# 128 rows of B's output weights by transfers of 5, 3 and 4 partitions

## The chip, the cores and the metric

The kernel runs on one core of a Trainium2 chip. Its time is the device time of one execution in microseconds (us). Before the change the median of 3 runs is 246.3 us (246.22 to 246.44). The profile is of one more execution; its span, from its first instruction to its last, is 245.2 us, and all positions below count from the start of that span.

## The reference

Two independent decode steps of attention, A and B, with one query token each; the two output rows are put side by side. For A only the last 2,048 of the 8,192 cached positions count, for B all of them.

```python
# per side: x [1,1,576], k_cache and v_cache [1,16,8192,128], wq [576,4096], wo [4096,576]
q = (x @ wq).reshape(B, Sq, Hq, Dh)              # 32 heads of 128, two for each cached head
scores = einsum("bhqd,bhkd->bhqk", q, k) * Dh ** -0.5
p = softmax(scores)
o = einsum("bhqk,bhkd->bhqd", p, v)
out = o.reshape(B, Sq, 4096) @ wo                # [1, 1, 576] for each side
```

All inputs are bf16. Nearly all the work is to read 102.8 MB once from HBM.

## The kernel before

**Loads.** Every large input goes through one ring in SBUF, `ring`, of 72 x 1,024 bf16 elements in each of 128 partitions. The helper `place` takes the next stretch of the ring and makes the load wait for the last use of what lay there. All loads are issued by SyncE (SP) in one order: wq of A and B, then K and V of eight units (four units of four cached heads for A, four for B), and at last wo. Each is one transfer over 128 partitions, and the profile's DMA records show it as 8 packets (one for each partition) on each of 16 DMA engines, each engine's share closed by a 4-byte packet that counts the semaphore up by one. An engine works through its packets in order, so the loads queue up behind one another by tens of us.

**Attention.** For each unit VectorE (DVE) turns slabs of K (line 350), TensorE (PE) makes the scores (line 367; a unit of A has a mask matmul of 4 partitions in front, line 359), ScalarE (ACT) takes the exponential (line 406), DVE turns that (lines 414 and 418), and PE multiplies by V (line 431), as the slabs land. Line 447 folds the result into `ob`.

**The end.** Lines 482 to 499 divide o by the softmax's sums and turn it, so that `oP[p, P, k]` holds number 32p + k of side P's o. wo has the same layout: partition p holds the 32 rows 32p to 32p + 31. One "row k" of the ring is thus 128 rows of wo, one in each partition, 576 elements (1,152 bytes) each. Line 229 loads wo: A's in one transfer of 32 rows, B's in five transfers of 17, 8, 4, 2 and 1 rows (`NWO`, line 34). For each row, PE makes two matmuls (line 510) with one column of `oP` as the stationary side: 320 output columns into one partition of the PSUM bank `fb`, 256 into another. A uses partitions 0 and 32 of `fb`, B 64 and 96. A matmul group waits for its own transfer and comes in program order: F0.0 (A, 32 rows), then F1.0 to F1.4 (B, 17, 8, 4, 2 and 1 rows). When a side is done, ACT (line 519) and DVE (line 521) copy its two sums to `outsb`, and SP stores 1,152 bytes (line 523). The store of A's row is issued behind all loads, and so is B's, which ends the program.

**Order.** Each engine runs its own list in program order; `op` adds an instruction with the names that it waits for, `load` a transfer with its semaphore.

Of the kernel before, what the change touches and what calls it, by code (L numbers as in the profile page):

```python
# [4 lines left out]
BF16 = mybir.dt.bfloat16  # L5
# [6 lines left out]
HQ = 32  # L12
G = 16
DH = 128
DM = 576
# [5 lines left out]
NQ = G // 4  # L21
# [8 lines left out]
N0 = 320  # L30
RING = 72 * 1024
NSEM = 24
NKT = 3
NWO = [[32], [17, 8, 4, 2, 1]]


class Prog:
# [9 lines left out]
    def op(self, eng, fn, deps=(), name=None):  # L47
        self.ops[eng].append((fn, tuple(deps), name, None))
        if name is not None:
            assert name not in self.where, name  # L50
            self.where[name] = (eng, len(self.ops[eng]) - 1)

    def load(self, eng, fn, sem, value, deps=(), name=None, step=16):
        self.ops[eng].append((fn, tuple(deps), None, (sem, step)))
        if name is not None:
            assert name not in self.dma, name
            self.dma[name] = (sem, value)
# [40 lines left out]
def bass_concat_heads__sliding_block_cached__gqa_block_cached__decode_kernel(nc, A_x, A_k_cache, A_v_cache, A_wq, A_wo,  # L98
                         B_x, B_k_cache, B_v_cache, B_wq, B_wo, out):
    xs, ks, vs = [A_x, B_x], [A_k_cache, B_k_cache], [A_v_cache, B_v_cache]  # L100
    wqs, wos = [A_wq, B_wq], [A_wo, B_wo]
# [4 lines left out]
    ring = nc.alloc_sbuf_tensor("ring", [128, RING], BF16)  # L106
    ktb = nc.alloc_sbuf_tensor("ktb", [128, NKT * SLAB], BF16)
    ident = nc.alloc_sbuf_tensor("ident", [128, 128], BF16)
# [33 lines left out]
    on = nc.alloc_sbuf_tensor("on", [128, 2, HQ], BF16)  # L142
    oq = nc.alloc_sbuf_tensor("oq", [128, 2, HQ], BF16)
    oP = nc.alloc_sbuf_tensor("oP", [128, 2, HQ], BF16)
    warm = nc.alloc_sbuf_tensor("warm", [128, 8], F32)
    outsb = nc.alloc_sbuf_tensor("outsb", [1, 2 * DM], BF16)

# [3 lines left out]
    mb = nc.alloc_psum_tensor("mb", [128, 512], F32)  # L151
    ob = nc.alloc_psum_tensor("ob", [128, 512], F32)

    def view(t, free, offset, dims, parts=128, p0=0):
        return bass.AP(tensor=t, offset=p0 * free + offset, ap=[[free, parts], *dims])

    pg = Prog(nc)
    op, load = pg.op, pg.load
    s_x = [nc.alloc_semaphore("s_x%d" % i) for i in range(2)]
    s_ld = [nc.alloc_semaphore("s_ld%d" % i) for i in range(NSEM)]  # L160
    s_out = nc.alloc_semaphore("s_out")
    s_row = [nc.alloc_semaphore("s_row%d" % i) for i in range(2)]


    live, at, nload, uses_of = [], [0], [0], []

    def place(size, uses, issue, name):
        if at[0] + size > RING:
            at[0] = 0
        lo, hi = at[0], at[0] + size  # L170
        at[0] = hi
        deps = []
        for r in list(live):
            if r[0] < hi and lo < r[1]:
                deps += r[2]
                live.remove(r)
        n = nload[0]
        nload[0] += 1
        if n >= NSEM:
            deps += uses_of[n - NSEM]  # L180
        uses_of.append(list(uses))
        live.append((lo, hi, list(uses)))
        t = ring[:, lo:hi]
        load("sp", lambda e: issue(e, t), s_ld[n % NSEM], 16 * (n // NSEM + 1), deps=deps, name=name)
        return t
# [39 lines left out]
    for P in range(2):  # L225
        k0 = 0
        for c, kk in enumerate(NWO[P]):
            src = wos[P].rearrange("(p k) n -> p (k n)", k=HQ)[:, k0 * DM:(k0 + kk) * DM]
            wo_at[P, c] = place(kk * DM, ["F%d.%d" % (P, c)], lambda e, t, src=src: e.dma_start(t, src),
                                "wo%d.%d" % (P, c))  # L230
            k0 += kk

    def slab(kind, i, s):

        parts = kv_at[kind, i]
        per = nslab[i] // len(parts)
        return parts[s // per][:, s % per * SLAB:(s % per + 1) * SLAB], "%s%d.%d" % (kind, i, s // per)
# [6 lines left out]
       deps=["id0"], name="ident")  # L244
# [12 lines left out]
    op("pool", lambda e: e.memset(zb[:], 0.0), name="zb0")  # L257
    op("pool", lambda e: e.tensor_copy(mkr[:], view(ident, 128, 0, [[0, 128], [1, 4]], 4)), deps=["ident"], name="mkr")
    op("pool", lambda e: e.memset(pts[:], 0.0), name="pts0")
    for c in range(2):  # L260
        op("dve", lambda e, c=c: e.tensor_reduce(par[:, c:c + 1], view(identf, 128, c, [[2, 64]]), AX.X, ALU.add),
           deps=["identf"], name="par%d" % c)
# [3 lines left out]
    for P in range(2):  # L266
        op("dve", lambda e, P=P: e.tensor_copy(  # L267
            view(xdup, 256, 128 * P, [[2, 64], [1, 2]], parts=1),
            view(xrow, 2 * DM, P * DM + 512, [[1, 64], [0, 2]], parts=1)), deps=["x%d" % P], name="xd%d" % P)
        for k in range(5):  # L270
            def mm(e, P=P, k=k):
                if k < 4:
                    lhsT = view(xrow, 2 * DM, P * DM + k, [[4, 128]], parts=1)
                else:
                    lhsT = xdup[0:1, P, :]
                return e.matmul(banks[2 * P + k // 4][:, (k % 4) * 128:(k % 4 + 1) * 128], lhsT=lhsT,  # L276
                                rhs=onesb[0:1, :], start=True, stop=True)
            op("pe", mm, deps=["x%d" % P, "onesb", "xd%d" % P], name="xT%d.%d" % (P, k))
        op("dve", lambda e, P=P: e.tensor_copy(
            xrep[:, P, 0:4, :].rearrange("p k m -> p (k m)"), banks[2 * P][:, :]), deps=["xT%d.3" % P], name="xr%d.0" % P)  # L280
        for c in range(2):
            op("dve", lambda e, P=P, c=c: e.tensor_scalar(
                xrep[:, P, 4 + c, :], banks[2 * P + 1][:, 0:128], par[:, c:c + 1], None, ALU.mult),
                deps=["xT%d.4" % P, "par%d" % c], name="xr%d.%d" % (P, 1 + c))
# [3 lines left out]
       deps=["identf"], name="clsb")  # L288
    op("dve", lambda e: e.tensor_reduce(clsa[:], view(identf, 128, 0, [[1, 8], [8, 16]]), AX.X, ALU.add),
       deps=["identf"], name="clsa")  # L290
    op("dve", lambda e: e.tensor_reduce(sel[:], view(identf, 128, 0, [[1, 32], [32, 4]]), AX.X, ALU.add),
       deps=["identf"], name="sel")
# [6 lines left out]
    for P in range(2):  # L299
        for n in range(8):  # L300
# [3 lines left out]
            def mm(e, P=P, n=n, bank=bank):  # L304
# [8 lines left out]
               name="qmm%d.%d" % (P, n))  # L313
            op("act", lambda e, u=u, bank=bank: e.activation(qsb[:, u % 4, :], bank[:, :], ACT.Copy),  # L314
               deps=["qmm%d.%d" % (P, n)] + (["qT%d" % (u // 2 - 2)] if u >= 4 else []), name="qe%d" % u)
            if n % 2:
# [3 lines left out]
                    deps=["qe%d" % (u - 1), "qe%d" % u] + (["z0.%d" % i for i in range(4)] if P else []),  # L320
                    name="qT%d" % (u // 2))
        for b in range(4):
            if P == 1:
# [3 lines left out]
                    deps=["qT%d" % u for u in range(4, 8)] + ["zb0"], name="z1.%d" % b)  # L327
            else:
# [3 lines left out]
                    deps=["qT%d" % u for u in range(4)] + ["za0"], name="z0.%d" % b)  # L332
# [4 lines left out]
    k0 = [sum(nslab[:i]) for i in range(NU)]  # L337
# [117 lines left out]
    for i in range(NU):  # L455
        n = nslab[i + 1] if i + 1 < NU else 0
# [18 lines left out]
        for s in range(nslab[i]):  # L475
# [13 lines left out]
                                start=True, stop=True),  # L489
       deps=["lsel", "lselA", "nb%d" % last, "mr%d" % last], name="L")  # L490
# [3 lines left out]
        deps=["rl", "O%d" % last], name="on")  # L494
    op("dve", lambda e: e.transpose(oq[:].rearrange("p c k -> p (c k)"), on[:].rearrange("p c k -> p (c k)")),
       deps=["on"], name="oq")
    op("pe", lambda e: e.matmul(mb[:, 64:128], lhsT=perm[:, :], rhs=oq[:].rearrange("p c k -> p (c k)"),
                                start=True, stop=True), deps=["oq", "rl", "perm"], name="pm")
    op("dve", lambda e: e.tensor_copy(oP[:].rearrange("p c k -> p (c k)"), mb[:, 64:128]), deps=["pm"], name="oP")


    fb = qb[0]
    for P in range(2):
        k0 = 0
        for c, kk in enumerate(NWO[P]):
            def mm(e, P=P, c=c, k0=k0, kk=kk):
                for k in range(kk):
                    for n in range(2):
                        r, lo, hi = 32 * (2 * P + n), n * N0, N0 + n * (DM - N0)
                        ins = e.matmul(fb[r:r + 1, 0:hi - lo], lhsT=oP[:, P, k0 + k:k0 + k + 1],  # L510
                                       rhs=wo_at[P, c][:, k * DM + lo:k * DM + hi],
                                       start=(k0 + k == 0), stop=(k0 + k == HQ - 1))
                return ins
            op("pe", mm, deps=["wo%d.%d" % (P, c), "oP", "exp%d" % (NQ - 2)], name="F%d.%d" % (P, c))
            k0 += kk
        done = "F%d.%d" % (P, len(NWO[P]) - 1)
        r, lo = 64 * P, P * DM

        load("act", lambda e, r=r, lo=lo: e.activation(outsb[0:1, lo:lo + N0], fb[r:r + 1, 0:N0], ACT.Copy),
             s_row[P], 2, deps=[done], name="f%d" % P, step=1)  # L520
        load("dve", lambda e, r=r, lo=lo: e.tensor_copy(outsb[0:1, lo + N0:lo + DM], fb[r + 32:r + 33, 0:DM - N0]),  # L521
             s_row[P], 2, deps=[done], step=1)
        load("sp", lambda e, lo=lo: e.dma_start(out[0, 0:1, lo:lo + DM], outsb[0:1, lo:lo + DM]),
             s_out, 16 * (P + 1), deps=["f%d" % P], name="out%d" % P)
# [31 lines left out]
```

## Time and profile before

| what | us |
|---|---|
| median of 3 runs | 246.3 (246.22 to 246.44) |
| span of the profiled execution | 245.2 |
| first load issued | 0.7 |
| issue of A's wo | 208.37 |
| A's wo landed, first matmul of line 510 | 232.32 |
| copies of A's row (lines 519, 521) | 239.75 |
| copies of B's row | 243.65 |
| store of B's row issued | 244.11 |

The DMA engines are busy nearly all the time: queue 1, which holds all loads, has packets in flight for 97.9% of 16 engines' span. The busy shares of the engines are PE 70%, DVE 53%, ACT 10%, POOL 3%. Two other queues carry instructions for the engines' sequencers: 7 packets of 16 KB and 2 of 8 KB within the span.

In the views, "x16" counts instructions, an arrow in brackets names what ended a wait, and PEclk is the granted share of TensorE's full clock, 1.00 or 0.50 here.

### The profile page before, as it was taken

How to read it: one execution, taken by the hardware profiler on the slowest of the kernel's cores; microseconds unless marked ns; L12 is line 12 of the kernel's file. 1: busy time of each engine (PE TensorE's matmuls, PEld its weight loads, DVE VectorE, ACT ScalarE, POOL GpSimd, SP SyncE). 2: the span in 40 equal slices, each digit the busy share in tenths (PEclk: the TensorE clock that was granted, in tenths of full speed). 3: DMA queues.
4: the chain of work that ended last, by engine and by line, in shares of the span. 5: the costliest groups of instructions: out<-in, count | busy, mean ns of one | idle time of the engine just before them, and what ended most of it. 6: DMA issues, size and time to landing. Idle time of an engine off the chain costs nothing.

```text
span 245.2 us, 2253 instructions
## 1 busy us (share of the span) xinstructions
PE 172.3 (70%) x960; PEld 71.8 (29%) x961; DVE 129.1 (53%) x162; ACT 24.3 (10%) x52; POOL 8.2 (3%) x15
## 2 busy tenths in 40 slices
PE   0269967787867994889582869945579939257197
PEld 0124422224433222432130523211423213213154
DVE  0422547667789986699501699810679920500201
ACT  2004540021201000100000100000010000200001
POOL 8400000000000000000000000000000000000000
PEclk9999995789999997569957578989657985677559
DMA  7999999999999999998999999999999999999994
GB/s 267 420 457 410 437 428 425 433 428 457 440 430 387 468 428 428 452 470 385 406 428 425 438 476 428 438 406 425 438 466 460 395 406 430 428 438 409 430 407 158
DMA packets 4481, 102.90 MB, mean 420 GB/s; under 512 B 500, under 2 KB 632, under 8 KB 1144
## 3 DMA queue, kind: packets, MB, share of 16 engines
q1 hardware_dynamic: 4468, 102.76, 97.9%
q8 instruction: 7, 0.11, 0.2%
q14 instruction: 2, 0.02, 0.0%
q10 hardware_dynamic: 4, 0.00, 0.0%
HBM read 102.76 MB, written 0.00 MB: 419 GB/s over the span
## 4 chain that ended last, share of the span: by engine, by line
DMA 55%; PE 29%; DVE 12%; ACT 2%; issue 2%; SPq 0%; DVEq 0%
DMA ring<-in_B_v_cache_dram 40%; DMA ring<-in_A_wo_dram 10%; DVE ktb L350 9%; PE vb L431 8%; DMA ring<-in_A_wq_dram 5%; PE qb L367 5%; PE qb L510 5%; PE sb L310 5%; PE qb L310 4%; ACT psb L406 1%; DVE pta L414 1%; PE ob L447 1%; PE sb L367 1%; PE qb L359 1%; PE mb L397 1%
## 5 line engine op out<-in xcount | busy, mean ns | idle before, releaser
L350 DVE STREAM_TRANSPOSE ktb<-ring 128x1024 int32<-128x1024 int32 x80 | 92.8, 1211 | 29.5 <-DMA ring<-in_B_k_cache_dram 28.3
L367 PE MATMUL sb<-ktb,zb 128*128 128x512 bf16 x256 | 76.0, 437 | 23.7 <-DVE ktb L350 21.1
L367 PEld LDWEIGHTS sb<-ktb,zb 128*128 128x128 bf16 x256 | 23.4, 106 | 72.4 <-DVE ktb L350 45.9
L431 PE MATMUL vb<-ring,pts 128*32 128x512 bf16 x256 | 24.7, 567 | 18.5 <-DMA ring<-in_B_v_cache_dram 14.4
L367 PE MATMUL qb<-ktb,za 128*128 128x512 bf16 x64 | 19.4, 449 | 2.8 <-DVE ktb L350 2.8
L431 PEld LDWEIGHTS vb<-ring,pts 128*32 128x32 bf16 x256 | 9.0, 134 | 33.6 <-DMA ring<-in_B_v_cache_dram 16.7
L438 ACT ACTIVATE xo<-vb 128x512 f32<-128x512 f32 x8 | 4.8, 597 | 129.4 <-PE vb L431 129.4
L418 DVE STREAM_TRANSPOSE pts<-psb 32x512 bf16<-32x512 bf16 x16 | 11.3, 703 | 9.5 <-ACT psb L406 9.3
L510 PE MATMUL qb<-ring,oP 128*1 128x256 bf16 (+1 forms) x128 | 11.3, 340 | 4.0 <-DMA ring<-in_A_wo_dram 4.0
L317 DVE STREAM_TRANSPOSE ktb<-qsb 128x512 int32<-128x512 int32 x8 | 5.7, 711 | 15.0 <-ACT qsb L314 15.0
L310 PE MATMUL sb<-ring,xrep 128*128 128x512 bf16 x40 | 11.4, 442 | 2.7 <-DMA ring<-in_A_wq_dram 2.7
L447 PEld LDWEIGHTS ob<-sel,xo 128*128 128x128 f32 x64 | 10.9, 244 | 3.8 <-ACT xo L438 2.2
L447 PE MATMUL ob<-sel,xo 128*128 128x8 f32 x64 | 10.1, 285 | 1.2 <-ACT xo L438 1.2
L367 PEld LDWEIGHTS qb<-ktb,za 128*128 128x128 bf16 x64 | 6.1, 109 | 13.4 <-issue 5.8
L310 PE MATMUL qb<-ring,xrep 128*128 128x512 bf16 x39 | 9.5, 393 | 0.0
L510 PEld LDWEIGHTS qb<-ring,oP 128*1 128x1 bf16 x128 | 7.0, 93 | 8.3 <-DMA ring<-in_A_wo_dram 4.1
L521 DVE CAST outsb<-qb 1x256 bf16<-1x256 f32 x2 | 0.8, 420 | 14.7 <-PE qb L510 14.7
L491 DVE RECIPROCAL rl<-mb 128x64 f32<-128x64 f32 x1 | 0.6, 558 | 12.3 <-PE mb L488 12.3
L276 PE MATMUL sb<-onesb,xrow 1*128 1x128 bf16 x4 | 0.6, 298 | 9.2 <-DVE xdup L267 9.2
L392 DVE TENSOR_REDUCE mr<-mb 1x8 f32<-1x128 f32 x8 | 1.9, 240 | 9.5 <-PE mb L384 9.5
L310 PEld LDWEIGHTS sb<-ring,xrep 128*128 128x128 bf16 x40 | 4.3, 109 | 8.6 <-issue 5.3
L314 ACT ACTIVATE qsb<-sb 128x512 bf16<-128x512 f32 x8 | 4.8, 597 | 19.1 <-PE sb L310 19.1
(65 smaller groups left out, 68.8 us busy)
## 6 DMA issues: line engine op xcount, KB each, us to landing
ring<-in_B_k_cache_dram SPq DMA_DIRECT2D x8, 4096.0 KB, 24.5
ring<-in_A_k_cache_dram SPq DMA_DIRECT2D x4, 2048.0 KB, 30.5
ring<-in_A_v_cache_dram SPq DMA_DIRECT2D x4, 2048.0 KB, 25.4
ring<-in_B_v_cache_dram SPq DMA_DIRECT2D x2, 4096.0 KB, 23.8
ring<-in_A_wo_dram SPq DMA_DIRECT2D x1, 4608.0 KB, 23.9
ring<-in_A_wq_dram SPq DMA_DIRECT2D x1, 4096.0 KB, 12.5
ring<-in_B_wq_dram SPq DMA_DIRECT2D x1, 4096.0 KB, 22.6
ring<-in_B_wo_dram SPq DMA_DIRECT2D x1, 2448.0 KB, 29.3
```

What stands on the lines that cost most here:

```text
L310: ins = e.matmul(bank[:, :], lhsT=lhsT, rhs=o, start=(k == 0), stop=(k == 4))
L314: op("act", lambda e, u=u, bank=bank: e.activation(qsb[:, u % 4, :], bank[:, :], ACT.Copy), deps=["qmm%d.%d" % (P, n)] + (["qT%d" % (u // ...
L317: op("dve", lambda e, u=u, n=n: e.transpose(ktb[:, (n - 1) * 512:(n + 1) * 512].bitcast(I32), qsb[:, u % 4 - 1:u % 4 + 1, :].rearrange("p ...
L350: op("dve", lambda e: e.transpose(kt.bitcast(I32), src.bitcast(I32)), deps=[landed] + (["S%d" % (k - NKT)] if k >= NKT else Z), name="T%d. ...
L359: e.matmul(bank[:, :], lhsT=mkl[:].rearrange("p a h r -> p (a h r)"), rhs=mkr[:].rearrange("p q h -> p (q h)"), start=True, stop=False)
L367: ins = e.matmul(bank[:, :], lhsT=lhsT, rhs=view(ktb, KT, (k % NKT) * SLAB + 64 * c + v, [[128, 16], [2, 32]]), start=(side == "B" and s = ...
L397: op("pe", lambda e: e.matmul(mb[:, 128:129], lhsT=mexp[0:1, :], rhs=onesf[0:1, 0:1], start=True, stop=True), deps=["mx%d" % i, "ones"], n ...
L418: op("dve", lambda e, b=b: e.transpose(view(pts, NB * 128, 2 * b, [[8, 16], [128, NB], [1, 2]], 32, 32 * b), psb[32 * b:32 * b + 32, :]), ...
L431: ins = e.matmul(vbank[i][32 * j:32 * j + 32, :], lhsT=lhsT, rhs=src[:, 512 * j:512 * j + 512], start=(s == 0), stop=(s == nslab[i] - 1))
L438: op("act", lambda e: e.activation(xo[:, c, :], vbank[i][:, :], ACT.Copy), deps=["V%d.%d" % (i, nslab[i] - 1)] + (["O%d" % (i - 1)] if i e ...
L447: ins = e.matmul(ob[:, at:at + 8], lhsT=xo[:, c, 128 * t:128 * t + 128], rhs=sel[:, 8 * t:8 * t + 8], start=(t == 0), stop=(t == 3))
L510: ins = e.matmul(fb[r:r + 1, 0:hi - lo], lhsT=oP[:, P, k0 + k:k0 + k + 1], rhs=wo_at[P, c][:, k * DM + lo:k * DM + hi], start=(k0 + k == 0 ...
```

## The change

B's wo is no longer loaded as 32 rows of 128 partitions, but as 31 of them (16, 8, 4, 2 and 1), and what was the last row, k = 31 (the rows 32p + 31 of wo, one for each p), is loaded by nine small transfers of its own. Each of these goes to only a few partitions, in steps of four: four transfers of 5 partitions with 5 rows each (partitions j, j + 4, ... j + 16 for j = 0 to 3), four of 3 partitions with 2 rows each, and one of 4 partitions (0 to 3) with 1 row each: 100 + 24 + 4 = 128 rows, in the first 20 partitions. They lie in 8 slots: five slots hold 20 rows, two hold 12, one holds 4 (`XK`). They are issued by SP between A's wo and B's.

The numbers of o that belong to these rows stand in one column of `oP`, `oP[:, 1, 31]`, one in each partition. Nine copies on GpSimd (POOL) near the start cut selection matrices `selx` out of the identity; eight matmuls (`oXm`, 1 output column each) move the 128 numbers to partitions 0 to 19, and three copies on DVE bring them to SBUF as `oX`. Before B's other rows, PE then makes 2 matmuls for each of the 8 slots (`Fx`), over 20, 12 or 4 partitions, into the same two partitions of `fb`.

```diff
-NWO = [[32], [17, 8, 4, 2, 1]]
+NWO = [[32], [16, 8, 4, 2, 1]]
+
+XWO = [(j, 0, 5, 5) for j in range(4)] + [(j, 5, 2, 3) for j in range(4)] + [(0, 7, 1, 4)]
+XAT = [sum(a * b for _, _, a, b in XWO[:i]) for i in range(len(XWO))]
+XK = [20] * 5 + [12] * 2 + [4]
+XS, XP = len(XK), XK[0]
...
+        if P == 0:
+            def issue(e, t, i):
+                j, s0, ns, ne = XWO[i]
+                row, src = HQ * DM, wos[1]
+                src = bass.AP(tensor=src.tensor, offset=src.offset + XAT[i] * row + (HQ - 1) * DM,
+                              ap=[[ns * row, ne], [row, ns], [1, DM]])
+                step = 4 if ns > 1 else 1
+                return e.dma_start(bass.AP(tensor=ring, offset=j * RING + xw_at + s0 * DM,
+                                           ap=[[step * RING, ne], [DM, ns], [1, DM]]), src)
+            xw = place(XS * DM, ["Fx"], lambda e, t: issue(e, t, 0), "xw.0")
+            xw_at = at[0] - XS * DM
+            for i in range(1, len(XWO)):
+                load("sp", lambda e, i=i: issue(e, None, i), s_xw[i - 1], 16, name="xw.%d" % i)
...
+    for i, (j, s0, ns, ne) in enumerate(XWO):
+        step = 4 if ns > 1 else 1
+        op("pool", lambda e, i=i, j=j, s0=s0, ns=ns, ne=ne, step=step: e.tensor_copy(
+            view(selx, XS * XP, s0 * XP + j, [[step, ne], [XP, ns]]), view(ident, 128, XAT[i], [[ns, ne], [1, ns]])),
+           deps=["ident"], name="selx.%d" % i)
...
+    def spreadx(e):
+        for c in range(XS):
+            ins = e.matmul(mb[0:XK[c], 128 + c:129 + c], lhsT=selx[:, c, 0:XK[c]], rhs=oP[:, 1, HQ - 1:HQ], start=True, stop=True)
+        return ins
+    op("pe", spreadx, deps=["oP"] + ["selx.%d" % i for i in range(len(XWO))], name="oXm")
+    for c0, c1 in ((0, 5), (5, 7), (7, 8)):
+        op("dve", lambda e, c0=c0, c1=c1: e.tensor_copy(oX[0:XK[c0], c0:c1], mb[0:XK[c0], 128 + c0:128 + c1]),
+           deps=["oXm"], name="oX.%d" % c0)
...
+        if P == 1:
+            def mmx(e):
+                for k in range(XS):
+                    for n in range(2):
+                        r, lo, hi = 32 * (2 + n), n * N0, N0 + n * (DM - N0)
+                        ins = e.matmul(fb[r:r + 1, 0:hi - lo], lhsT=oX[0:XK[k], k:k + 1], rhs=xw[0:XK[k], k * DM + lo:k * DM + hi],
+                                       start=(k == 0), stop=False)
+                return ins
+            op("pe", mmx, deps=["oX.0", "oX.5", "oX.7", "exp%d" % (NQ - 2)] + ["xw.%d" % i for i in range(len(XWO))], name="Fx")
```

More of the change, by code (lines that the diff above doesn't have):

```diff
@@ L144, in bass_concat_heads__sliding_block_cached__gqa_block_cached__decode_kernel @@
     oP = nc.alloc_sbuf_tensor("oP", [128, 2, HQ], BF16)
+    selx = nc.alloc_sbuf_tensor("selx", [128, XS, XP], BF16)
+    oX = nc.alloc_sbuf_tensor("oX", [XP, XS], BF16)
     warm = nc.alloc_sbuf_tensor("warm", [128, 8], F32)
@@ L160, in bass_concat_heads__sliding_block_cached__gqa_block_cached__decode_kernel @@
     s_ld = [nc.alloc_semaphore("s_ld%d" % i) for i in range(NSEM)]
+    s_xw = [nc.alloc_semaphore("s_xw%d" % i) for i in range(len(XWO) - 1)]
     s_out = nc.alloc_semaphore("s_out")
@@ L511, in mm @@
                                        rhs=wo_at[P, c][:, k * DM + lo:k * DM + hi],
-                                       start=(k0 + k == 0), stop=(k0 + k == HQ - 1))
+                                       start=(P == 0 and k0 + k == 0), stop=(k0 + k == sum(NWO[P]) - 1))
                 return ins
```

## The prediction

> **What bounds the kernel now.** I read the chain of waits first, in order of time; its last pieces (start, length, what) are:
>
> ```profile
> 168.52 33.42 DMA ring<-in_B_v_cache_dram
> ...
> 201.98 6.34 PE vb L431 x63
> ...
> 208.37 23.91 DMA ring<-in_A_wo_dram
> ...
> 232.32 11.31 PE qb L510 x94
> ...
> 243.65 0.43 ACT outsb L519
> ```
>
> Up to 232.3 transfers set the pace. From there the chain never goes back to one: it runs along PE through line 510 to the end. So I looked at whether PE or the last transfers end later, first by the issues (KB, and us from issue to landing):
>
> ```profile
> ring<-in_B_wo_dram SPq DMA_DIRECT2D x1, 2448.0 KB, 29.3
> ring<-in_B_wo_dram SPq DMA_DIRECT2D x1, 1152.0 KB, 31.6
> ring<-in_B_wo_dram SPq DMA_DIRECT2D x1, 576.0 KB, 32.5
> ```
>
> SP issues these at 208.74 and then every 0.475 us, so they land at about 238.1, 240.8 and 242.2; the trace's completion counts put the last two (2 rows and 1 row) at 242.92 and 243.27. Against that stands the timeline (start, length; in brackets idle time and what ended it):
>
> ```profile
> 242.96 0.09 PEld L510 LDWEIGHTS qb<-ring,oP 128*1 128x1 bf16 x4 [0.21 <-DMA ring<-in_B_wo_dram]
> 243.31 0.08 PEld L510 LDWEIGHTS qb<-ring,oP 128*1 128x1 bf16 x2 [0.26 <-DMA ring<-in_B_wo_dram]
> 243.65 0.43 ACT L519 ACTIVATE outsb<-qb 1x320 bf16<-1x320 f32 x1 [3.47 <-PE qb L510]
> ```
>
> The weight loads of the last 3 rows do wait for transfers, but hardly the matmuls: PE's matmuls of line 510 run on without a gap. By the trace's starts, B's first row begins at 239.01, and full-clock rows follow each 0.136 us (320 columns; the 256-column half runs beside it). Row 32 would then start at 239.01 + 31 x 0.136 = 243.22; it started at 243.31. PE has 0.09 us to spare: at the end transfers and PE are in a tie.
>
> Then windows over the final transfers (busy time by engine, PEclk, DMA share):
>
> ```profile
> 240.40:240.80 0.40, 0.40 (x11) 0.24 (x8) 0.00 (x0) 0.00 (x0) 0.00 (x0) 1.00 0.96 372
> 240.80:241.20 0.40, 0.40 (x11) 0.24 (x8) 0.00 (x0) 0.00 (x0) 0.00 (x0) 1.00 0.63 248
> 241.20:241.60 0.40, 0.40 (x11) 0.24 (x8) 0.00 (x0) 0.00 (x0) 0.00 (x0) 1.00 0.53 207
> 241.60:242.00 0.40, 0.40 (x10) 0.24 (x7) 0.00 (x0) 0.00 (x0) 0.00 (x0) 1.00 0.49 187
> 242.00:242.40 0.40, 0.40 (x8) 0.32 (x6) 0.00 (x0) 0.00 (x0) 0.00 (x0) 1.00 0.36 130
> 242.40:242.80 0.40, 0.40 (x9) 0.31 (x5) 0.00 (x0) 0.00 (x0) 0.00 (x0) 1.00 0.10 35
> ```
>
> Half of the 16 DMA engines run dry near 241.0, the rest at 242.0 to 242.9: the sixteen counts of the last transfer come at 240.92 to 241.72 for eight engines and 242.25 to 243.27 for eight. The late ones are those that also carried an instruction fetch. That unevenness is what the change acts on.
>
> Last, PE's clock at the end:
>
> ```profile
> 231.39:234.80 3.41, 2.48 (x22) 1.88 (x24) 0.50 0.98 419
> 234.80:238.21 3.41, 3.41 (x31) 1.61 (x27) 0.50 0.96 401
> 238.21:241.63 3.41, 3.41 (x62) 2.45 (x60) 1.00 0.88 358
> ```
>
> PE starts line 510 at half clock, 0.267 us a row, and gets the full clock at 238.21, after one window that it filled.
>
> **The change part by part.**
>
> *Transfers.* One row fewer in each engine's share: 8 packets of 1,152 bytes, 0.35 us by the last transfer, which lands 0.35 us after the one before it. In their place come 128 packets on few engines. A transfer of 5 partitions has at most 5 shares; that these are engines 0 to 4, 3 partitions 0 to 2, and 4 partitions 0 to 3, the trace can't show. What it has are two one-partition transfers, x of A and of B, which went through one engine, the same for both and not a late one. On that reading engines 0 to 2 get 20 + 8 + 1 = 29 packets, engine 3 gets 21, engine 4 gets 20: with 0.044 us each and less the 0.35, +0.93, +0.57 and +0.53 us. If all five are among the early eight, they end by 241.72 + 0.93 = 242.65, the late ones at 243.27 - 0.35 = 242.92, and the last landing gains 0.35 us. If one of engines 0 to 2 is late, the last landing loses up to 0.93. The Trainium skill, "DMA: Bandwidth & Descriptors", in its section on why a DMA increments its semaphore by 16, says that such a transfer runs on the lowest-numbered k engines, k the largest divisor up to 16 of the slowest dimension; that gives the same 29, 21 and 20, and no run here yet shows a k of 3 to 5.
>
> *SP.* Nine more issues at 0.475 us move B's five wo issues from 208.74 by 4.3 us, the last to about 214.9. The cover is the queue: the first packet of B's wo starts at 229.45, so 16 us are left; without it the 4.3 us would be paid. The ring has room: the new stretch overlaps only what wo of A has waited for, so no wait is added.
>
> *POOL and DVE.* Nine small copies follow POOL's last work (8.9 us) and are needed at 228.6. `oXm` and three copies come after `oP` (228.35 + 0.22): eight matmuls at about 0.11 us (the one-partition row of line 276 at half clock) and three copies at about 0.2 (the row of `oP`), done near 230.5. PE waits for A's wo until 232.32 anyway; were that cover gone, they would cost about 2 us.
>
> *PE.* 8 slots come, 1 row goes: +7 rows x 0.136 = 0.95 us at full clock, less 0.09 to spare: **+0.86**. A matmul over 4 partitions takes the time of its columns (half-clock rows of line 276 with one partition: 128 columns in 0.107), so short slots are not cheaper. Ten more semaphore waits stand before `Fx` (PE's wait at 228.6 took 0.05); PE's sequencer runs some 14 rows ahead, which hides them; bare, 0.5 us.
>
> *Array shape.* PE goes from 128 partitions to 20 and back. Nearest row: line 359 (4 partitions) starts at 55.33, line 367 (128) at 55.64, 0.32 us for 512 columns, where the next ones follow after 0.22. So 0.10 a change, two changes: **+0.20** (bounds 0 to 0.20, since the way into the small shape has no row). Besides, B's first row now starts 0.40 us before A's last (239.01 against 239.41), on other columns of the array. If the other shape forbids that, up to 0.40 is lost; nothing decides, so I take half: **+0.20**. The Trainium skill, "TensorEngine Tiling (Array Packing)", key properties, says that a change of tiling mode drains the engine; by that all 0.40 would be lost, 0.20 more than in the sum.
>
> *Clock.* In the whole trace PEclk changes only on a grid of 3.413 us, and nothing in the kernel ties that grid to the first matmul of line 510. A window filled to over nine tenths is what mostly raises it. With the first matmul at 232.32 the rise comes between 235.5 and 238.9; here it came at 238.21. Each us earlier gains half a us of rows: from -1.37 to +0.33 against this execution, mean **-0.52**. The old kernel would gain nothing by it, since its end waits for transfers. The Trainium skill, "TensorE: Matmul & The Clock Gate", says that the window runs free and does not restart with a kernel; with a grid fixed as in this profile the 0.52 would not be taken off.
>
> *Sum.* 0.86 + 0.20 + 0.20 - 0.52 = +0.74 us. In the profiled execution's own phase it would be 1.26 on its span of 245.2. The median of the runs lies 1.1 above the span, the part outside it, which stays: 246.3 + 0.74 = **247.0 us**. As the gap between transfers and PE goes, the last landing (242.92) will no longer be what is late; PE's last row is.
>
> **The rivals.**
>
> *The landing is what counts (not slower).* If the clock rises early (by about 235.6), PE keeps up and the end follows the last landing: -0.35, **245.95**. For it: the transfers' unevenness is real, and 0.35 is the most that it can give, as late engines lose 8 packets. Against: it needs a rise 2.6 us before the profile's, nearly all of the range.
>
> *Late engines among the first five.* Their 29 packets land last: +0.93, **247.2**, whatever PE does, and at most about that unless PE is later still. For it: eight of 16 engines are late. Against: the one engine that one-partition transfers show is early. With 20 or 21 packets it would be +0.55, 246.85.
>
> *The change does not shift the load.* If the small transfers spread over all engines, the landing stays at 243.27; PE decides all the same: 247.0.
>
> *PE at its worst.* Profile's clock or later, and all overlap lost: 0.86 + 0.20 + 0.40 + 0.1 to 0.33, **247.9**.
>
> **How the numbers follow.** The forecast (PE's rows set the end, between 246.4 and 247.5) has 0.55, landing 0.15, late engines 0.18 (unshifted load is in the forecast), PE at its worst 0.12. About 0.2%, 0.5 us, is what can be told from no change. Slower by more: two thirds of the forecast (0.37), nearly all of late engines (0.16) and all of the worst (0.12), 0.65. Faster by more than 0.5 has no mechanism, since the landing gives 0.35 at most; 0.05 for that being mis-sized. Same: 0.30. The range reaches from the landing's 245.9 to 247.7, leaving out half the worst case and a little below.
>
> **What would show it.** Right: the new lines of `Fx` and the old ones run without a gap on PE to the end, and B's last matmul starts 0.5 us or more after the last transfer has landed. Transfers: the last landing's sixteen counts lie closer, late ones 0.35 earlier. Shape: a gap of over 0.3 us at the borders of `Fx`. Wrong: B's last weight load still waits for its transfer by 0.2 us or more, or PE waits before `Fx`.

## The result and the profile after

The changed kernel takes 247.41 us (median of 6 runs, 246.71 to 248.19) against 246.31 (246.22 to 246.44): 1.0042 of the time before, 95% interval 1.0027 to 1.0057. It is slower by 1.1 us, and its runs spread over 1.5 us where the old kernel's spread over 0.2. The profiled execution after is one of the quickest: 246.76 us, span 245.1, no longer than the span before. So the two profiles side by side show nearly no loss, and the reading has to say what differs from run to run.

The chain of waits after, its last pieces (start, length, what; line 554 is the old 510, line 545 the new slots):

```profile
232.08 0.04 issue
232.12 5.75 PE qb L554 x44
237.88 1.18 PE qb L545 x14
239.06 4.40 PE qb L554 x49
243.46 0.02 issue
243.48 0.43 ACT outsb L563
```

As before, the chain stays on PE from the landing of A's wo to the end, now through the slots. The windows say why this execution got away with it (busy time by engine, PEclk, DMA share, GB/s):

```profile
231.29:234.70 3.41, 2.58 (x23) 1.88 (x24) 0.00 (x0) 0.00 (x0) 0.00 (x0) 0.50 1.03 438
234.70:238.11 3.41, 3.41 (x50) 2.04 (x48) 0.19 (x1) 0.19 (x1) 0.00 (x0) 1.00 0.95 395
238.11:241.53 3.41, 3.41 (x55) 2.41 (x51) 0.23 (x1) 0.24 (x1) 0.00 (x0) 1.00 0.93 377
```

The full clock came at 234.70, a whole window earlier than in the profile before (238.21), and saved PE 3.51 / 2 = 1.75 us of rows. That is just enough for the added rows, and the end of the timeline looks like the old one (in brackets the idle time and what ended it):

```profile
242.78 0.09 PEld L554 LDWEIGHTS qb<-ring,oP 128*1 128x1 bf16 x4 [0.18 <-DMA ring<-in_B_wo_dram]
243.13 0.08 PEld L554 LDWEIGHTS qb<-ring,oP 128*1 128x1 bf16 x2 [0.26 <-DMA ring<-in_B_wo_dram]
243.48 0.43 ACT L563 ACTIVATE outsb<-qb 1x320 bf16<-1x320 f32 x1 [5.13 <-PE qb L554]
```

By the signs that the prediction named, this execution speaks against it: B's last weight load still waits 0.26 us for its transfer, and the last row starts at 243.14, right behind the last landing (243.09), not 0.5 us or more after it.

The transfers, in the windows over their end, are more even than before, but no earlier:

```profile
240.80:241.20 0.40, 0.40 (x10) 0.25 (x8) 0.00 (x0) 0.00 (x0) 0.00 (x0) 1.00 0.75 291
241.20:241.60 0.40, 0.40 (x10) 0.24 (x8) 0.00 (x0) 0.00 (x0) 0.00 (x0) 1.00 0.74 288
241.60:242.00 0.40, 0.40 (x8) 0.24 (x6) 0.00 (x0) 0.00 (x0) 0.00 (x0) 1.00 0.70 256
242.00:242.40 0.40, 0.40 (x9) 0.38 (x8) 0.00 (x0) 0.00 (x0) 0.00 (x0) 1.00 0.28 98
```

The DMA share of the stretch from 240.8 to 242.0 rose from about 0.55 to 0.73, since the early engines now work on. Yet the last landing is at 243.09, 11.01 us after A's wo (232.08); before it was 243.27 and 232.28, 10.99. The transfers gained nothing.

One more number stands beside the span: the time of a run less its span. It is 1.32 us in the old kernel (29 executions, 1.27 to 1.36) and 1.63 to 1.71 in five of six executions of the new one (2.49 in the sixth). So of 1.1 us lost, 0.35 lies outside the span, where the prediction put nothing.

### The profile page after: what moved, and what is told of

Its sections match the earlier page's. It is cut to its first block, busy times and chain, and to the rows that moved or that the text cites. A ratio compares the mean times of both kernels' runs of the same rounds, so it can differ in the third digit from the quotient of the medians.

```text
span 245.1 us, 2324 instructions
## 1 busy us (share of the span) xinstructions
PE 171.0 (70%) x983; PEld 71.1 (29%) x983; DVE 130.0 (53%) x165; ACT 24.3 (10%) x52; POOL 9.3 (4%) x24
## 4 chain that ended last, share of the span: by engine, by line
DMA 55%; PE 29%; DVE 12%; ACT 2%; issue 1%; SPq 0%; DVEq 0%
DMA ring<-in_B_v_cache_dram 40%; DMA ring<-in_A_wo_dram 10%; DVE ktb L376 9%; PE vb L457 8%; DMA ring<-in_A_wq_dram 5%; PE qb L393 5%; PE sb L336 4%; PE qb L554 4%; PE qb L336 4%; ACT psb L432 1%; DVE pta L440 1%; PE ob L473 1%; PE sb L393 1%; PE qb L385 1%; PE mb L423 1%
## 5 line engine op out<-in xcount | busy, mean ns | idle before, releaser
L393 PE MATMUL sb<-ktb,zb 128*128 128x512 bf16 x256 | 75.1, 431 | 23.0 <-DVE ktb L376 20.1
L554 PE MATMUL qb<-ring,oP 128*1 128x256 bf16 (+1 forms) x126 | 10.2, 312 | 3.3 <-DMA ring<-in_A_wo_dram 3.3
L473 PEld LDWEIGHTS ob<-sel,xo 128*128 128x128 f32 x64 | 10.0, 227 | 3.6 <-ACT xo L464 2.3
L473 PE MATMUL ob<-sel,xo 128*128 128x8 f32 x64 | 9.3, 274 | 1.2 <-ACT xo L464 1.2
```

What stands on the lines that cost most here:

```text
L393: ins = e.matmul(bank[:, :], lhsT=lhsT, rhs=view(ktb, KT, (k % NKT) * SLAB + 64 * c + v, [[128, 16], [2, 32]]), start=(side == "B" and s = ...
L473: ins = e.matmul(ob[:, at:at + 8], lhsT=xo[:, c, 128 * t:128 * t + 128], rhs=sel[:, 8 * t:8 * t + 8], start=(t == 0), stop=(t == 3))
```

## The experiments

Each was timed in 5 rounds against the kernel before on the same chip. "Outside" is the median of time less span.

| run | time | before | ratio (95%) | span | outside |
|---|---|---|---|---|---|
| e1 transfers alone | 246.35 | 246.26 | 0.9996 to 1.0014 | 245.0 | 1.32 |
| e2 8 rows alone | 246.64 | 246.26 | 1.0010 to 1.0028 | 245.3 | 1.34 |
| e3 8 slots alone | 247.52 | 246.26 | 1.0030 to 1.0062 | 246.2 | 1.31 |
| e4 more instructions | 246.32 | 246.26 | 0.9993 to 1.0010 | 245.0 | 1.36 |
| e5 fetch at the end | 246.55 | 246.47 | 0.9996 to 1.0018 | 245.1 | 1.36 |
| e6 after, fetch earlier | 247.29 | 246.47 | 1.0025 to 1.0049 | 245.6 | 1.69 |
| e7 after, 128 partitions | 246.78 | 246.47 | 1.0007 to 1.0036 | 245.3 | 1.37 |
| e8 after, clock up | 246.94 | 246.47 | 1.0007 to 1.0025 | 245.3 | 1.68 |
| e9 before, clock up | 246.37 | 246.43 | 0.9989 to 1.0006 | 245.0 | 1.33 |
| e10 after, one more on POOL | 247.85 | 246.43 | 1.0036 to 1.0076 | 245.9 | 1.67 |
| e11 three partitions | 246.93 | 246.43 | 1.0015 to 1.0038 | 245.4 | 1.52 |
| e12 after, one more on DVE | 247.33 | 246.43 | 1.0023 to 1.0051 | 246.0 | 1.33 |

**e1: the transfers without PE's part.** `NWO` and the nine loads as in the change; no `selx`, `oXm`, `oX`, `Fx`, so the 128 products of row 31 are left out of the result.

```diff
-NWO = [[32], [17, 8, 4, 2, 1]]
+NWO = [[32], [16, 8, 4, 2, 1]]
...
+            xw = place(XS * DM, ["F1.0"], lambda e, t: issue(e, t, 0), "xw.0")
+            xw_at = at[0] - XS * DM
+            for i in range(1, len(XWO)):
+                load("sp", lambda e, i=i: issue(e, None, i), s_xw[i - 1], 16, name="xw.%d" % i)
```

> Row 31 of B's wo is loaded by the nine small transfers, but nothing reads it: its 128 products are left out of the sum, with the selection matrices, oXm, oX and Fx. PE has one row less than before. If PE's added rows are the cost (my theory), the time falls to the landing of the last transfer: 0.2 to 0.35 us under the kernel before, with little spread. If the small transfers themselves cost (late engines among the first five, a longer issue, or their semaphores), it stays 0.5 us or more above. The profile after had its last landing only 0.18 us earlier than before, and A's wo 0.20 earlier; if that is the transfers' real worth, the gain counted from the landing of A's wo is near 0.

Measured: no difference that can be told (the interval is 0.9996 to 1.0014). The transfers cost nothing, and they gain nothing even with one row less on PE. The end of its timeline:

```profile
242.74 0.09 PEld L529 LDWEIGHTS qb<-ring,oP 128*1 128x1 bf16 x4 [0.37 <-DMA ring<-in_B_wo_dram]
243.09 0.09 PEld L529 LDWEIGHTS qb<-ring,oP 128*1 128x1 bf16 x2 [0.27 <-DMA ring<-in_B_wo_dram]
```

Here PE waits for transfers at the end, and the last landing (243.05) is 11.07 us behind that of A's wo (231.98). The completion counts in the trace after tell why. The transfers have 5, 3 and 4 counts, one for each share. In the four of 5 partitions one share lands 0.6 us behind the others (231.56, 231.79, 232.03 and 232.26); at that pace its count in the transfer of 4 is the one at 232.47, and in those of 3 it has none. That is an engine which has part in 5 and 4 partitions but not in 3, and one of the late ones, since by the same pace its count of A's wo is the one at 231.31. (The trace doesn't name the engines; the counts are put together by their distances.) Its 21 packets took 232.47 - 231.31 = 1.16 us, 0.055 each with their closing packets, not 0.044. It was 0.77 us ahead of the last engine, and +1.16 - 0.35 = +0.81 makes it the last itself. What the true last engine gained, this one used up. Nor was 0.35 to be had: the next counts of the last transfer, 242.85 and 242.86, are 10.77 us behind A's wo, so without that share the landing would have gained about 0.2 us. What keeps the rest is not shown.

**e2 and e3: PE's part without the transfers.** The kernel before, with 8 rows of zeros between A's rows and B's, over 128 partitions (e2) or 20 (e3):

```diff
+        if P == 1:
+            def mmz(e):
+                for k in range(8):
+                    for n in range(2):
+                        r, lo, hi = 32 * (2 + n), n * N0, N0 + n * (DM - N0)
+                        ins = e.matmul(fb[r:r + 1, 0:hi - lo], lhsT=zb[0:128, 0, 0, 0:1], rhs=wo_at[0, 0][0:128, k * DM + lo:k * DM + hi],
+                                       start=(k == 0), stop=False)
+                return ins
+            op("pe", mmz, deps=["wo0.0", "oP", "exp%d" % (NQ - 2)], name="Fz")
```

> All transfers as before; between A's rows and B's, PE makes 8 more rows over 128 partitions with a stationary column of zeros (16 matmuls of 320 and 256 columns that add 0 to B's sums). If PE's rows and the clock set the end: +8 x 0.136 - 0.09 = +1.0 us in an execution whose clock rises as late as in the profile before, less by half of each us that it rises earlier, so single runs from -0.0 to +1.3 and a median of +0.3 to +0.8. If PE has room after all: no change. If what costs is the code (32 more PE instructions, a further instruction fetch), the span stays and the time outside it grows by some 0.5 us.

> As the run with 8 rows of zeros, but over 20 partitions in place of 128. If the change of the array's shape costs 0.1 us each way and the overlap with A's last rows (up to 0.4 us), this is 0.2 to 0.6 us slower than that run at an equal rise of the clock, and the trace shows a gap between A's last row and the first slot. If shape costs nothing, the two agree but for the clock.

Measured: +0.38 us for the rows, +1.26 for the slots, both with a wide spread like the changed kernel's (246.3 to 247.34 and 246.36 to 247.87), so that a median of few executions says little to some tenths: the slots alone lie above the whole change. By luck the two profiled executions had their clock rise at the same place (236.00 and 235.97), so they can be laid side by side. PE's pieces at the border, e2 first:

```profile
237.86 0.38 PE L510 MATMUL qb<-ring,zb 128*1 128x320 bf16 x3
237.98 0.30 PE L519 MATMUL qb<-ring,oP 128*1 128x320 bf16 x1
237.99 0.36 PE L510 MATMUL qb<-ring,zb 128*1 128x320 bf16 x2
238.12 0.30 PE L519 MATMUL qb<-ring,oP 128*1 128x320 bf16 x1
```

```profile
232.18 6.35 PE L519 MATMUL qb<-ring,oP 128*1 128x320 bf16 x64 [2.79 <-DMA ring<-in_A_wo_dram]
238.46 1.24 PE L510 MATMUL qb<-ring,zb 20*1 20x320 bf16 x16
239.63 4.51 PE L519 MATMUL qb<-ring,oP 128*1 128x320 bf16 x64
```

In e2, rows of zeros (line 510) start from 237.86 on, between A's last rows (line 519, the last at 238.26); B's own rows begin at 238.94. In e3 nothing overlaps: the first slot starts 0.23 us after A's last row (238.23) and B's first row 0.22 after the last slot (239.40), where 0.136 is a row's pace. B's rows begin 0.69 us later. That is the price of the shape: with 128 partitions the rows on other columns of the array run ahead of A's last by 0.40 us, with 20 they do not.

**e4, e5, e6: instruction fetches.** The trace after has an eighth fetch of 16 KB, at 244.43, behind PE's last matmul. I took it for the cause of the 0.35 us outside the span. e4 and e5 add 32 and 25 matmuls of one column to the old kernel, e6 adds 32 to the new one, where PE waits for A's wo. The edit of e4 (e5 has 25 in the loop, e6 writes `qb[1]`):

```diff
+    def idle(e):
+        for k in range(32):
+            ins = e.matmul(mb[0:1, 200:201], lhsT=zb[:, 0, 0, 0:1], rhs=zb[:, 0, 0, 0:1], start=True, stop=True)
+        return ins
+    op("pe", idle, deps=["oP"], name="idle")
```

> The kernel before with 32 matmuls of one column each after oP, where PE waits for A's wo: 64 more PE instructions and no more work at the end. In the profile after, an eighth fetch of 16 KB starts at 244.43, behind PE's last matmul, and the time outside the span is 1.65 us in five of six runs. If that fetch holds up the end of the program: the same fetch near 244, span as before (245.2) and +0.4 to +0.6 us in the time. If it is harmless: no change, and the time outside the span comes from something else, such as the added semaphores.

> The kernel before with 25 matmuls of one column after oP (in place of 32): 50 more PE instructions, so that the program has as many as the changed kernel, within one or two, and the eighth fetch of 16 KB falls on the last rows, not 2 us before them. If a fetch that is still under way when the program ends is what lengthens the time outside the span: span as before (244.9 to 245.0), time outside it 1.65 to 1.7 us in place of 1.32, median 246.6. If that time comes from the added transfers or semaphores: 1.32 outside, 246.3.

> The changed kernel with 32 matmuls of one column after its oXm, which moves the eighth fetch some 64 instructions ahead, out of the last rows. By the theory of the fetch at the end: time outside the span back to 1.32, and the median 0.35 us lower, near 247.05, with the same spread. If the 0.35 comes from something else, it stays at 247.4.

Measured: the fetch moved as meant (241.42 in e4, 243.18 in e5, 241.49 in e6), and the time outside did not follow it: 1.36, 1.36, 1.69. In e5 the fetch ended at 244.58, still ahead of the end of the span; what settles it are e6 and e8 (fetch at 241.80), where it is long over and the time outside stays at 1.69 and 1.68. That theory fell. e6's profile is of use for another thing. It caught a late clock (windows: busy time by engine, PEclk, DMA share):

```profile
230.74:234.16 3.42, 2.09 (x26) 1.60 (x24) 0.00 (x0) 0.00 (x0) 0.00 (x0) 0.50 1.00 418
234.16:237.57 3.41, 3.41 (x31) 1.64 (x28) 0.00 (x0) 0.00 (x0) 0.00 (x0) 0.50 0.95 397
237.57:240.98 3.41, 3.41 (x48) 2.15 (x47) 0.42 (x1) 0.43 (x1) 0.00 (x0) 1.00 0.95 389
```

and the end that goes with it:

```profile
243.72 1.11 PE L560 MATMUL qb<-ring,oP 128*1 128x320 bf16 x10
244.00 0.49 PEld L560 LDWEIGHTS qb<-ring,oP 128*1 128x1 bf16 x6
244.88 0.43 ACT L569 ACTIVATE outsb<-qb 1x320 bf16<-1x320 f32 x1 [5.05 <-PE qb L560]
```

No weight load waits for a transfer any more; the last row starts at 244.54, 1.36 us after the last landing (243.18), and the span is 246.5. This is the forecast's mechanism in full sight, which the first profile after happened to miss.

**e7: the shape kept.** In the changed kernel, `oX` over 128 partitions with zeros; the slots' other partitions hold old data of the ring, times zero.

```diff
-    oX = nc.alloc_sbuf_tensor("oX", [XP, XS], BF16)
+    oX = nc.alloc_sbuf_tensor("oX", [128, XS], BF16)
...
+    op("pool", lambda e: e.memset(oX[:], 0.0), name="oX0")
...
-                        ins = e.matmul(fb[r:r + 1, 0:hi - lo], lhsT=oX[0:XK[k], k:k + 1], rhs=xw[0:XK[k], k * DM + lo:k * DM + hi],
+                        ins = e.matmul(fb[r:r + 1, 0:hi - lo], lhsT=oX[:, k:k + 1], rhs=xw[:, k * DM + lo:k * DM + hi],
```

> The changed kernel with oX widened to 128 partitions (zeros below the 20, 12 or 4 in use) and the slots' matmuls over all 128, so that the array keeps its shape. At an equal rise of the clock the run with 8 rows of 20 partitions ended 0.69 us after the one with 128. By that the first slot starts again some 0.4 us ahead of A's last row, and the span falls by up to 0.7 where PE's rows set the end, less where the landing does: median 246.8 to 247.0 with the fetch at the end still in it. If shape is not the cause: 247.4.

Measured: 246.78, 0.31 above the kernel before in place of 1.1. The slots (line 546) start 0.40 us ahead of A's last row (line 555) again:

```profile
238.54 0.38 PE L546 MATMUL qb<-ring,oX 128*1 128x320 bf16 x3
...
238.94 0.30 PE L555 MATMUL qb<-ring,oP 128*1 128x320 bf16 x1
```

About 0.3 us of the fall lies outside the span, where the time is 1.37 in place of 1.7; that I hadn't foreseen.

**e8 and e9: the clock.** PE is given matmuls without use while it waits for A's wo: 8 of 512 columns in the changed kernel (e8); 2 behind line 488 and 5 behind `oP` in the kernel before (e9).

```diff
+    def warmup(e):
+        for k in range(8):
+            ins = e.matmul(qb[1][:, :], lhsT=perm[:, :], rhs=psb[:, :], start=True, stop=True)
+        return ins
+    op("pe", warmup, deps=["oP"], name="warmup")
```

> The changed kernel with 8 matmuls of 512 columns and 128 partitions after oXm, into a bank that nothing uses by then, so that PE is busy from 228.9 to about 232.1, when A's wo lands. If PE's clock is what makes the changed kernel slow and uneven: the clock rises some 3 us earlier, line 554 runs at 0.136 us a row for most of A's rows, the last row waits for its transfer in every run, the spans fall together to 244.9 to 245.1 and the median to 246.2 to 246.4 (the 16 further instructions also take the eighth fetch off the end). If rows are not the bound: 247.0 or more, as uneven as before.

> The kernel before with 2 matmuls of 512 columns after line 488 and 5 after oP, in PE's idle time before A's wo, so that the clock rises earlier. By the prediction the old end waits for its transfers and would gain nothing by a faster PE: the median within 0.1 us of before, the last matmul still starting right behind the last landing. If the old kernel had been held up by PE's clock as well: 0.1 to 0.4 us faster.

Measured: e8 246.94, its spread cut from 1.5 us to 0.6 (246.58 to 247.16); with the 0.35 outside taken off, 0.1 us remains above the kernel before. PE's pieces show the clock risen and the filling too long:

```profile
230.22 3.49 PE L539 MATMUL qb<-psb,perm 128*128 128x512 bf16 x8
233.64 4.51 PE L560 MATMUL qb<-ring,oP 128*1 128x320 bf16 x64
```

A's rows begin 1.3 us behind their landing (232.37), and still end in 4.51 us instead of the 7.4 that they took in the profile before. e9 is no different from the kernel before: with a clock at its full from 233.68 on, PE stands still for 0.75 us before B's first transfer, and the last weight load waits as ever:

```profile
238.09 5.32 PE L519 MATMUL qb<-ring,oP 128*1 128x320 bf16 x64 [0.75 <-DMA ring<-in_B_wo_dram]
...
243.10 0.08 PEld L519 LDWEIGHTS qb<-ring,oP 128*1 128x1 bf16 x2 [0.27 <-DMA ring<-in_B_wo_dram]
```

The old end is the transfers', not PE's.

**e10 and e12: the time outside the span.** One more instruction that nobody reads, on POOL (e10) or on DVE (e12), in the changed kernel:

```diff
+    op("pool", lambda e: e.memset(pad[:], 0.0), name="pad0")
```

```diff
+    op("dve", lambda e: e.tensor_copy(pad[:, :], oP[:, 0, 0:8]), deps=["oP"], name="pad0")
```

> The changed kernel with one more instruction on POOL near the start (a memset of 8 columns that nobody reads). The time outside the span is 1.68 us in the changed kernel and in two kernels made from it, and 1.3 in the one with oX over 128 partitions, which has one more memset on POOL and one more wait on DVE; in the trace the last four counts of the closing barrier come 0.47 us after the five before them, in place of 0.10. If the place at which POOL's program ends decides: 1.32 us outside, median 247.05. If it is DVE's, or the slots of 12 and 4 partitions: 1.68 and 247.4.

> The changed kernel with one more instruction on DVE (a copy of 8 columns of oP that nobody reads), where DVE waits for oXm. The time outside the span was 1.67 to 1.69 us in the four kernels with 184 recorded DVE instructions, 1.32 to 1.37 in those with 181 or 185, and one more on POOL left it. If the length of DVE's program is what sets the late end of the closing barrier: 185 instructions, 1.32 to 1.37 outside, median about 247.05 with the changed kernel's spread. If the slots of 20, 12 and 4 partitions are: 1.68 and 247.4.

Measured: POOL's leaves it at 1.67, DVE's brings it back to 1.33 (four of five executions; one had 2.82, and such single values occur in other kernels too). So the 0.35 us hangs on DVE's program, which the change made three instructions longer, and one more undoes it; that it is the number of instructions which counts, and not something else that goes with it, is not shown. What happens there in those 0.35 us stays open: the trace shows only that the last four counts of the closing barrier come 0.47 us after the five before them where DVE has 184 recorded instructions, and 0.10 to 0.11 after them where it has 181, 182 or 185. e12's median (247.33) did not fall with it, since its few executions happened to have long spans (245.4 to 246.3).

**e11: a version that should gain.** Only transfers of 3 partitions, 4 of them with 8 rows each; 32 rows in one transfer of 32 partitions; slots over 128 partitions; PE kept busy as in e9.

```diff
...
+                ap = [[XS * row, 3], [row, XS], [1, DM]] if i < XN else [[row, 32], [1, DM]]
...
+                    dst = bass.AP(tensor=ring, offset=i * RING + xw_at, ap=[[4 * RING, 3], [DM, XS], [1, DM]])
+                else:
+                    dst = bass.AP(tensor=ring, offset=at_p * RING + xw_at, ap=[[RING, 32], [1, DM]])
...
```

> A version that would gain if my reading of the engines is right: only transfers of 3 partitions (engines 0 to 2, all early in the traces; engine 3, which is a late one, gets nothing more), four of them with 8 rows each, for 96 of the 128 rows; the other 32 rows by one transfer of 32 partitions; all slots over 128 partitions with zeros, and PE kept busy before A's wo. Late engines lose 6 packets of 0.044 us, engines 0 to 2 gain 26. The last landing comes 0.25 us earlier than before and the last row follows it: 0.15 to 0.3 us under the kernel before, if the time outside the span stays at 1.32. If small transfers can't gain at all, or PE is still the bound: the same or slower.

Measured: 246.93, 0.5 above. PE is no longer the bound, since it waits for each of B's transfers (0.45 us before line 560's matmuls at 240.88). The last landing is 10.84 us behind A's wo, 0.15 better than before, not 0.25: two of the three engines took 1.6 us for their 32 packets, and the counts at 243.25 and 243.26, close to the last at 243.31, fit their pace. But A's wo itself landed later (232.47), and 0.2 us more lie outside the span; why is open (DVE has 182 recorded instructions here, and the closing barrier shows 0.10, not 0.47). No version beat the kernel before.

## Why the prediction was right, point by point

**What bounds the kernel.** A tie of PE and transfers, held: e2 adds only PE work and is slower, e9 speeds PE up and gains nothing, e1 frees PE of a row and gains nothing. That PE's rows then set the end held in part. Four kernels have the change's rows and slots and no filling for the clock: the changed one, e6, e10 and e12. In their profiles the end waits for the last transfer in two (the changed kernel's, and e12 with 0.27 us), PE comes 0.13 us behind the landing in one (e10) and 1.36 in one (e6). Of their 27 executions 18 have a span longer than any of the old kernel's 89. In the quick executions it is as the rival of the landing says, except that the landing gains nothing.

**Transfers.** The forecast took no gain from them, rightly, though the landing was to come 0.35 earlier if all of engines 0 to 4 were early. One of them, engine 3 on the prediction's reading, was late: the rival's mechanism, but with 21 packets on an engine that had 0.77 us in hand, so that the landing moved by 0.02 and not by 0.55. The sixteen counts do lie closer (2.03 us from first to last, 2.35 before), but the late ones are not 0.35 earlier. The nesting of the shares (3 partitions within 4 within 5) agrees with the rule of the Trainium skill, "DMA: Bandwidth & Descriptors", section on why a DMA increments its semaphore by 16, that the lowest-numbered engines are used.

**SP.** Hidden, as said, though the issues were longer than in the sum: a 5-partition issue took 0.71 to 0.96 us, not 0.475, and the issue of the last two transfers stood for 8.1 and 2.9 us. They were out at 227.9, not 214.9, and still over 10 us before their turn.

**Rows.** The pace behind +0.86 stands: the slots follow one another at 0.136 us, as full rows do (e2 and e3). 8 rows alone cost 0.38 at the median, where an earlier clock hides part of them (in e2's profile it rises at 236.00, and the last weight load waits for its transfer again). The added waits were hidden, as said, though PE's sequencer was eight or nine rows ahead and not 14: it worked through them from 236.25 to 236.73, and the first slot started at 237.81.

**Array shape.** +0.40 in the sum, 0.69 measured (e3 against e2). The overlap was not halved but lost, and its loss is not 0.40: rows that ran 0.40 ahead of A's last now start 0.23 behind it, 0.63, and the way back adds 0.09. The gap of over 0.3 us that was named as the sign does not show. The Trainium skill, "TensorEngine Tiling (Array Packing)", key properties, has the array drained on a change of mode; the trace agrees, with those 0.23 and 0.22 in place of 0.136. The larger price that I gave beside the sum was the better one.

**Clock.** -0.52 in the sum; the range of rises was too late by nearly a us. A window that PE filled to 76% (2.58 of 3.41 us) was enough in the profile after, and 73% (2.48) was not in the one before; I had asked for nine tenths. These two figures are no threshold: elsewhere in the profile before, a window filled to 3.41 of 3.41 us (176.77 to 180.19) was followed by half clock, so that the busy time alone does not decide it. But the rise can come from 234.7 on, as it did in two of the four profiles of the new kernel and its variants with the same rows (234.70, 234.72, 235.18, 237.57). That the window is free from run to run, as the Trainium skill, "TensorE: Matmul & The Clock Gate", says, agrees with the traces: counted from the span's start and taken modulo 3.413 us, the grid of the 14 profiles lies anywhere from 0.45 to 3.07. The spans fit that: the 27 executions of these four kernels spread from 245.0 to 246.6 with no gap over 0.2, median 245.8; the old kernel's 89 from 244.8 to 245.4, median 245.1.

**Sum.** Between the spans the loss is about 0.7 us (245.8 against 245.1; the changed kernel's own six executions have 245.35, too few to set against that), near the forecast's +0.74. That is luck, by two errors that cancel: the shape was 0.3 too small, and so what the early clock took off must have been some 0.3 too small as well (0.86 + 0.69 - 0.7 = 0.85 in place of 0.52; no run measures it by itself). The step that failed is the last, that the time outside the span "stays": it grew by 0.35, and by e10 and e12 that goes with DVE's program, not with the rows, the slots or the transfers. Without it the time would have been 247.06; with it, 247.41 is still within the range. (It is 1.32 in the old kernel, not the 1.1 of the sum, which set the median of the runs against one long span; the forecast does not hang on that.)

## What to carry to other kernels

Before moving bytes to idle DMA engines, find out by the completion counts which engines are idle, and count what the receiving side must do with pieces that no longer fill 128 partitions: here eight short rows cost PE as much time as eight full ones, 0.136 us each, and the change of shape another 0.69 us. Where a stretch of PE work follows an idle time, as here, its length differs from run to run with the place of the clock's window (A's rows took 7.4 us in the profile before, 5.75 in the one after), so a single profile may show the best or the worst of them. And compare the time less the span before explaining a change of some tenths of a us within it.

## What was not expected of the hardware

The issue of a transfer by SP stood for 8.1 us with about fifteen transfers under way, where no semaphore was waited for; in e11, with four transfers fewer, the last three stood for 3.2, 9.4 and 2.9 us, and the kernel before had none that did (0.43 each). With a DVE program of 184 recorded instructions the time outside the span was 0.35 us longer than with 181 or 185. And matmuls of one program that write other columns of the array started before earlier ones of theirs that were still waiting their turn: in the kernel before, B's first row at 239.01, ahead of A's last three (239.13 to 239.41).
